# Two slots of the last expert stage shared between two experts, 96 rows of one and 32 of the other

## The chip, the cores and the metric

The kernel runs on one core of a Trainium2 chip. The time is device microseconds of that core; the kernel before takes 881.44 us (median of three runs, 881.35 to 882.75). All arithmetic is in float32. A float32 matrix product is two passes in the trace: two weight loads (PEld) and two matmuls (PE) for one product in the code.

## The reference, cut to what matters

An attention block feeds a mixture of experts in which each row goes to exactly one of eight experts, and no row is dropped.

```python
# attention: batch 8, 8 heads, 576 positions, head size 64; a window of 32,
# in half of the heads with steps of 4
attn = softmax(where(mask, q @ k.T / 8, -1e9));  x = (attn @ v)   # -> 4608 rows of 512
# experts: 8, hidden 1024
logits = x @ w_gate
expert_idx = np.argmax(logits, axis=1)
gate_w = softmax(logits)[row, expert_idx]
for e in range(E):                       # lo, hi: the rows of expert e, sorted
    h = np.maximum(x_sorted[lo:hi] @ w1[e], 0.0)     # 512 -> 1024
    y_sorted[lo:hi] = h @ w2[e]                      # 1024 -> 512
out = gate_w[:, None] * y                # in the rows' own order
```

How many rows an expert gets is known only when the kernel has computed the logits.

## The kernel before, in words

The kernel is one program in which two streams of work are interleaved as the program is written out: attention, with routing after each batch, and the expert slots.

**Buckets.** After the attention of a batch, `route` finds the expert of each of its 576 rows and its place among that expert's rows (VectorE, and small products on TensorE), and GpSimd scatters the rows by indirect DMA into `bucket` in HBM, in which expert e has the rows from e x 4608 on (L158). A row is 514 numbers: 512 of x, the gate's weight, the number of the token. After the last batch, GpSimd also writes blank rows behind the last row of each expert.

**Slots.** A slot is 128 consecutive rows of one expert's bucket. An expert whose count is no multiple of 128 has a last slot that is only partly filled. The number of slots is at most `NSLOT` = 43; the first 36 (`SURE`) always run, the others stand under a branch (L733) on the number that the tables found. Slots are planned in seven stages, one after each batch from the second on: `tables(s)` counts, on one partition of VectorE, the whole slots that are ready, and writes for each slot of the stage its expert (`ex`), the first row in the bucket (`base`), and whether its weights differ from those two slots before (`new`). The last stage, from slot 24 on, takes all that is left, partly filled slots too: experts are sorted by slots left, the list is cut in two halves, and even slots take the first half, odd slots the second, so that one expert stays in one of the two weight buffers.

**A slot's work** (`moe`). `across` turns the slot's 128x512 rows with four transposes (L721) and a copy on VectorE (L723). The first product keeps 128x128 pieces of w1 stationary and streams the 128 turned rows, 32 products into two PSUM banks (L747); ScalarE (L757) and VectorE (L765) apply the relu and so have the hidden layer already turned. The second product keeps pieces of that stationary and streams 512 columns of w2, 8 products (L771). ScalarE scales by the gate (L775), and GpSimd scatters the result rows to `out` (L780). The transposes of the next slot stand between the two halves of the first product.

**Loads.** w1 and w2 of an expert are 2 MB each, and each has two buffers, for even and odd slots. `wanted` is the list of loads in order: rows and w1 of slot j once slot j-2 is past its first product, w2 once slot j-2 is done. They are all issued from SP's queue, in this order; an issue waits on SP until the buffer's last reader is done (slot j-2), and all behind it wait too. A weight DMA has a condition (L695): where `new` is 0 it moves nothing.

**Order.** `run_slots` and `run_routing` set the program order: steps of a slot have costs written by hand (0.93, 0.88, 0.5), routing and tables proceed by one `yield` each time slots have advanced by 2.0 once attention is over.

## Time and profile before

| | |
|---|---|
| median of three runs | 881.44 us |
| the profiled execution | 879.85 us |
| its span, first to last instruction | 878.0 us |
| granted TensorE clock, mean | 0.956 |
| TensorE busy | 805.5 us (92%) |
| VectorE, ScalarE, GpSimd busy | 289.3, 224.9, 145.3 us |
| first product L747 | 2496 passes, 307.7 us |
| second product L771 | 624 passes, 294.2 us |
| slots that run (L775) | 39, the last one's y at 859.39 us |
| HBM read, written | 216.56 MB, 22.07 MB |

A page gives, for each group of instructions, the line of the program, the engine, the output and inputs by their names, the shape, the count, the busy time and the mean duration of one in ns, and the idle time before it with what ended it. Passes on TensorE overlap, so the mean duration of one (279 ns for L747) is longer than the distance from one to the next. PEclk is the granted clock in 40 slices of the span (9 is 0.9 or more). A timeline row is start, duration, engine, line and count of merged instructions, all in us. The issue of a DMA on SP's queue is marked SPq.

### The profile page before, as it was taken

The page shows a single profiled execution, that of the slowest core. Times are in us where ns is not written, and L with a number is a line of the kernel's source. Part 1 is how long each engine was busy: PE and PEld are TensorE (multiplying, and loading weights), DVE is VectorE, ACT ScalarE, POOL GpSimd, SP SyncE. Part 2 cuts the span into 40 slices and gives each one's busy share as a digit, 9 for nine tenths or more (in the row PEclk, how much of TensorE's full clock was granted, in tenths as well). Part 3 has the DMA queues.
Part 4 walks back from the last instruction along what each step waited for, and adds up shares of the span by engine and source line. Part 5 has one row for each costly group of instructions (what it writes and reads, how often), then busy time and mean ns, then how long its engine had stood idle before and what let it go on. Part 6 is the DMA issues. An engine that isn't in the chain of part 4 may idle for free.

```text
span 878.0 us, 17811 instructions
## 1 busy us (share of the span) xinstructions
PE 805.5 (92%) x6830; PEld 602.8 (69%) x6830; DVE 289.3 (33%) x891; ACT 224.9 (26%) x823; POOL 145.3 (17%) x139
## 2 busy tenths in 40 slices
PE   5888779899999999998999899889999999999991
PEld 4766668676677677776777677556867677777770
DVE  3775867445433433343334412310101010101010
ACT  3665463431433133332323121000000000000000
POOL 0214323213110311122111210420000000000000
PEclk9978889899999999999999899979999999999996
DMA  9877489898996869784367256769911380649574
GB/s 195 178 162 150 135 265 305 200 322 259 277 343 208 286 165 291 283 254 158 74 216 252 84 201 232 278 221 332 320 41 49 125 313 27 234 136 333 205 253 176
DMA packets 145720, 187.41 MB, mean 213 GB/s; under 512 B 72222, under 2 KB 86174, under 8 KB 145632
## 3 DMA queue, kind: packets, MB, share of 16 engines
q1 hardware_dynamic: 135316, 164.56, 61.6%
q0 software_dynamic: 6832, 19.71, 6.4%
q10 hardware_dynamic: 3484, 1.96, 1.0%
q8 instruction: 57, 0.93, 0.4%
q14 instruction: 31, 0.25, 0.1%
HBM read 216.56 MB, written 22.07 MB: 272 GB/s over the span
## 4 chain that ended last, share of the span: by engine, by line
PE 50%; issue 33%; DVE 4%; ACT 3%; POOL 3%; DMA 3%; another core or an unknown queue 1%; POOLq 0%; SPq 0%
PE ph L747 16%; PE py L771 15%; PE xo L340 4%; PE scores L274 4%; PE weights L325 3%; ACT e L300 3%; POOL out_dram L780 2%; PE xrow L426 2%; PE turned L238 2%; PE logits L436 2%; DMA k<-in_k_dram 2%; PE turned L246 1%; PE xt L721 1%; DMA bucket<-rows,idx 1%; POOL bucket L158 1%
## 5 line engine op out<-in xcount | busy, mean ns | idle before, releaser
L747 PE MATMUL ph<-xt,w 128*128 128x128 f32 x2496 | 307.7, 279 | 1.4 <-issue 1.4
L747 PEld LDWEIGHTS ph<-xt,w 128*128 128x128 f32 x2496 | 293.8, 193 | 20.7 <-issue 17.7
L771 PE MATMUL py<-w,h 128*128 128x512 f32 x624 | 294.2, 608 | 8.1 <-issue 8.1
L771 PEld LDWEIGHTS py<-w,h 128*128 128x128 f32 x624 | 112.7, 193 | 120.9 <-issue 116.7
L300 ACT ACTIVATE e<-e,lo 128x96 f32<-128x96 f32 x288 | 103.8, 364 | 91.9 <-DVE lo L294 84.7
L780 POOL DMA_INDIRECT out_dram<-y,to x39 | 38.8, 994 | 422.2 <-ACT y L775 388.7
L775 ACT ACTIVATE y<-py,x 128x512 f32<-128x512 f32 x39 | 26.7, 686 | 273.6 <-PE py L771 166.0
L723 DVE COPY xt<-xt 128x512 f32<-128x512 f32 x40 | 27.6, 690 | 210.0 <-PE xt L721 208.2
L315 POOL TENSOR_TENSOR e<-e,rec 128x864 f32<-128x864 f32 x32 | 52.1, 1629 | 202.6 <-DVE rec L314 107.1
L327 DVE COPY eT<-weights 96x384 f32<-96x384 f32 x96 | 48.4, 547 | 61.7 <-PE weights L325 54.3
L285 DVE SCALAR_TENSOR_TENSOR e<-scores,cst 128x384 f32<-128x384 f32 (+1 forms) x128 | 46.8, 396 | 48.2 <-PE scores L274 39.9
L765 DVE TENSOR_SCALAR h<-ph 128x512 f32<-128x512 f32 x39 | 27.0, 692 | 98.5 <-PE ph L747 86.3
L340 PEld LDWEIGHTS xo<-eT,v 96*64 96x64 f32 x1216 | 41.9, 143 | 24.0 <-issue 11.8
L274 PE MATMUL scores<-kT,qT 64*64 64x96 f32 x1152 | 43.4, 279 | 14.4 <-issue 8.3
L340 PE MATMUL xo<-eT,v 96*64 96x64 f32 (+1 forms) x1216 | 48.6, 231 | 6.6 <-issue 3.7
L300 ACT ACTIVATION_READ_ACCUMULATOR e<-e,lo 128x1 f32 x288 | 54.5, 189 | 0.0
L158 POOL DMA_INDIRECT bucket<-rows,idx x48 | 44.5, 928 | 57.3 <-DVE idx L525 26.9
L274 PEld LDWEIGHTS scores<-kT,qT 64*64 64x64 f32 x1152 | 34.6, 154 | 26.1 <-issue 16.0
L757 ACT ACTIVATE h<-ph 128x512 f32<-128x512 f32 x39 | 23.2, 596 | 102.4 <-PE ph L747 102.4
L325 PE MATMUL weights<-ident,e 128*96 128x128 f32 x288 | 42.1, 297 | 4.5 <-POOL e L315 4.5
L325 PEld LDWEIGHTS weights<-ident,e 128*96 128x96 f32 x288 | 35.1, 138 | 11.8 <-issue 5.2
L294 DVE TENSOR_REDUCE lo<-e 128x9 f32<-128x864 f32 x32 | 33.6, 1051 | 0.9
(104 smaller groups left out, 449.4 us busy)
## 6 DMA issues: line engine op xcount, KB each, us to landing
w<-in_moe_w_dram SPq DMA_DIRECT2D x82, 2048.0 KB
x<-bucket SPq DMA_DIRECT2D x41, 257.0 KB
v<-in_v_dram SPq DMA_DIRECT2D x32, 192.0 KB
q<-in_q_dram SPq DMA_DIRECT2D x32, 144.0 KB
q<-in_q_dram SPq DMA_DIRECT2D x8, 576.0 KB
v<-in_v_dram SPq DMA_DIRECT2D x48, 96.0 KB
k<-in_k_dram SPq DMA_DIRECT2D x28, 144.0 KB
k<-in_k_dram SPq DMA_DIRECT2D x7, 576.0 KB
```

Source lines behind the costliest of these rows:

```text
L158: nc.gpsimd.indirect_dma_start(out=bucket, out_offset=bass.IndirectOffsetOnAxis(ap=idx, axis=0), in_=rows, in_offset=None, bounds_check=NR ...
L274: nc.tensor.matmul(sc[r][64 * c : 64 * c + 64, 96 * (i % 5) : 96 * (i % 5) + 96], lhsT=qT[rows, 64 * j : 64 * j + 64], rhs=kT[rows, first_ ...
L285: nc.vector.scalar_tensor_tensor(out=e[p0:p1, i : i + n].rearrange("p i k -> p (i k)"), in0=sc[r][p0:p1, cols], scalar=-SCALE, in1=const(f ...
L294: nc.vector.tensor_reduce(out=lo, in_=e, axis=AX, op=OP.min)
L300: nc.scalar.activation(out=e[:, n], in_=e[:, n], func=AF.Exp, bias=lo[:, n : n + 1], scale=-1.0, accum_out=den[:, n : n + 1],)
L315: nc.gpsimd.tensor_tensor(out=e, in0=e, in1=rec.unsqueeze(2).broadcast_to([128, 9, 96]), op=OP.mult)
L325: nc.tensor.transpose(tp[0:96, 128 * i : 128 * i + 128], e[:, a + i], ident)
L327: nc.vector.tensor_copy(eT, tp[0:96, 0:384])
L340: nc.tensor.matmul(xo[DH * h : DH * h + DH, at0 : at0 + nq], lhsT=vt[:, 2 * hl + r, j, :] if ty == 0 else vt[:, hl, j, DH * r : DH * r + D ...
L747: nc.tensor.matmul(ph[:, fi], lhsT=w1[:, c, 128 * f : 128 * f + 128], rhs=xt[:, c], start=c == 0, stop=c == 3,)
L771: nc.tensor.matmul(py, lhsT=h[:, f], rhs=w2[:, f], start=f == 0, stop=f == 7)
L780: i = nc.gpsimd.indirect_dma_start(out=out, out_offset=bass.IndirectOffsetOnAxis(ap=to, axis=0), in_=y, in_offset=None, bounds_check=N - 1 ...
```

## The change

Groups of 32 rows become the unit in which the tails of experts are counted. `pairs` looks for experts with a tail of exactly one group; up to two of them (as many as there are other tails to go with) are each paired with the expert that has the largest tail. A pair shares one slot: 96 rows (three groups) of the one, 32 of the other. The two places for such slots are fixed: slots 24+3 and 24+7. `mixing` puts the experts and first rows of these slots in place of what the tables had. Where no pair is found, the same program computes nothing but rows of the first expert in that slot. `NSLOT` becomes 41.

A mixed slot is computed the other way round: the turned rows are stationary in four pieces of 32 columns, and w1 of the group's expert is streamed, 512 columns at a time, so each group of 32 rows comes out on its own 32 partitions (`grouped`). The hidden layer then has to be turned (`turned_h`, four transposes and a copy, twice). The second product is grouped likewise. The second expert's weights lie in the other parity's buffer; they are loaded when the slot before is past it, and the slot after the mixed one loads its own weights when the mixed slot is past it. From slot 26 on, rows are fetched from ScalarE's queue, in a mixed slot with four DMAs of 32 rows. The small constants of the last stage come with a DMA of their own on ScalarE's queue into a tile that attention no longer needs. The two buffers of w1, and those of w2, become one tile with an index.

```diff
+G = 32
+KIND = (3, 3)
+NMIX = len(KIND)
...
-NSLOT = (N + E * 127) // 128
...
+NSLOT = _most_slots()
...
+MIX = (3, 7)
+STEP = MIX[1] - MIX[0]
+J0 = STAGES[-1][1]
+assert J0 + MIX[-1] < SURE
...
+        if last:
+            scratch = pool.tile([TT, NT, 4, DH], F32, tag="q0", name="scratch", bufs=1)
+            scratch = scratch.rearrange("p t h d -> p (t h d)")[0:1]
+            width = packed_last.shape[1]
+            nc.scalar.dma_start(
+                scratch[:, 0:width], nc.inline_tensor(packed_last, name="c_last").ap()
+            )
+            mix["const"] = lambda name: scratch[:, last_at[name][0] : sum(last_at[name])]
+            used_up = [width]
...
+        if last:
+            yield
+            yield from pairs(cnt, table)
+            ns = mix["ns"]
...
+            plan, lists = table("plan", 2 * K, NMIX + 1), table("lists", 2 * K)
+            nc.vector.tensor_tensor(
+                out=plan,
+                in0=mix["const"]("plan").rearrange("p (k m) -> p k m", m=NMIX + 1),
+                in1=mix["many"].unsqueeze(1).broadcast_to([1, 2 * K, NMIX + 1]),
+                op=OP.mult,
+            )
+            nc.vector.tensor_reduce(out=lists, in_=plan, axis=AX, op=OP.add)
...
+            yield from mixing(ex, base, new, table)
...
+    def pairs(cnt, table):
+        c31, qi, qf = table("c31", E, dt=I32), table("qi", 2, E, dt=I32), table("qf", 2, E)
+        nc.vector.tensor_scalar(c31, cnt[0:1], G - 1.0, None, op0=OP.add)
+        nc.vector.tensor_scalar(qi[:, 0], c31, 5, None, op0=OP.logical_shift_right)
+        nc.vector.tensor_scalar(qi[:, 1], c31, 7, None, op0=OP.logical_shift_right)
+        nc.vector.tensor_copy(qf, qi)
...
+        ones, n1 = table("ones", E), table("n1", 1)
+        has, some = table("has", E), table("tails", 1)
+        nc.vector.tensor_scalar(ones, u, 1.0, None, op0=OP.is_equal)
+        nc.vector.tensor_reduce(out=n1, in_=ones, axis=AX, op=OP.add)
+        nc.vector.tensor_scalar(has, u, 1.0, None, op0=OP.min)
+        nc.vector.tensor_reduce(out=some, in_=has, axis=AX, op=OP.add)
...
+        nc.vector.tensor_scalar(rb, mix["const"]("ends"), some, None, op0=OP.add)
+        nc.vector.tensor_tensor(out=valid, in0=ra, in1=rb, op=OP.is_lt)
+        nc.vector.scalar_tensor_tensor(
+            out=valid, in0=ra, scalar=n1, in1=valid, op0=OP.is_lt, op1=OP.mult
+        )
+        nc.vector.tensor_reduce(out=m, in_=valid, axis=AX, op=OP.add)
+        nc.vector.tensor_scalar(many, mix["const"]("many"), m, None, op0=OP.is_equal)
...
+        nc.vector.tensor_tensor(out=ns, in0=has, in1=qf[:, 1], op=OP.add)
+        nc.vector.tensor_tensor(out=ns, in0=ns, in1=paired, op=OP.subtract)
+        yield
+        mix.update(ns=ns, m=m, many=many, valid=valid, got=got)
...
+    def mixing(ex, base, new, table):
+        valid = mix["valid"]
...
+        other, newb = mixf[:, 0:NMIX], mixf[:, NMIX : 2 * NMIX]
+        instead(other, at(ex, MIX[0]), b[0], "inex")
+        instead(at(ex, MIX[0]), at(ex, MIX[0]), a[0], "inex")
+        nc.vector.tensor_copy(prev, exs[:, J0 - 2 : NSLOT - 2])
+        nc.vector.tensor_copy(at(prev, MIX[0] + 1), other)
+        nc.vector.tensor_tensor(out=newb, in0=other, in1=at(ex, MIX[0] - 1), op=OP.not_equal)
+        nc.vector.tensor_tensor(out=new, in0=ex, in1=prev, op=OP.not_equal)
...
+        for i, n in enumerate(KIND):
+            own = mix["const"]("own")[:, 4 * i : 4 * i + 4]
+            for x, g0, g1 in ((first, 0, n), (then, n, 4)):
+                nc.vector.tensor_scalar(
+                    begins[:, i, g0:g1], own[:, g0:g1], x[:, i : i + 1], None, op0=OP.add
+                )
+        mixi = mpool.tile([1, 6 * NMIX], I32, name="mixi", bufs=1)
+        nc.vector.tensor_copy(mixi, mixf)
+        mix["ints"] = mixi
...
-    w1s = [cpool.tile([128, 4, F], F32, name=f"w1_{i}") for i in range(2)]
-    w2s = [cpool.tile([128, 8, DM], F32, name=f"w2_{i}") for i in range(2)]
+    w1s = cpool.tile([128, 2, 4, F], F32, name="w1")
+    w2s = cpool.tile([128, 2, 8, DM], F32, name="w2")
+    mixed = {J0 + at0: i for i, at0 in enumerate(MIX)}
...
+        queue = nc.scalar if j >= J0 + 2 else nc.sync
+        if j in mixed:
+            for g in range(4):
+                a = 2 * NMIX + 4 * mixed[j] + g
+                at0 = queue.value_load(
+                    mix["ints"][:, a : a + 1], min_val=0, max_val=NROWS - G
+                )
+                read_bucket(queue.dma_start(x[G * g : G * g + G], bucket[ds(at0, G), :]), b)
+        else:
+            at0 = queue.value_load(basei[:, n : n + 1], min_val=0, max_val=E * CAP)
+            read_bucket(queue.dma_start(x, bucket[ds(at0, 128), :]), b)
+    def fetch_w(j, dst, src, other=False):
         _, n, exi, _, newi = where[j]
-        rv = nc.sync.value_load(exi[:, n : n + 1], min_val=0, max_val=E - 1)
+        if other:
+            i = mixed[j]
...
-            dst[j % 2], src[ds(rv, 1)].rearrange("o (c l) f -> l (o c) f", l=128), **kw
+            dst[:, (j + other) % 2], src[ds(rv, 1)].rearrange("o (c l) f -> l (o c) f", l=128), **kw
...
-        wanted += [(j, "x", 0, j - 1), (j, "w1", 0, j - 1), (j, "w2", 1, j - 1)]
+        x = (j, "x", 0, j - 1)
+        behind = j - (j - 1 not in mixed)
+        w = [(j, "w1", 0, behind), (j, "w2", 1, behind)]
+        if j - 1 in mixed:
+            wanted.insert(len(wanted) - 1, x)
+        else:
+            wanted.append(x)
+        wanted += w
+        if j in mixed:
+            wanted += [(j, "w1b", 0, j), (j, "w2b", 1, j)]
...
+            def grouped(out, lhsT, ws, cols, c, n, j=j):
+                for g in range(4):
+                    mine = slice(G * g, G * g + G)
+                    nc.tensor.matmul(
+                        out[mine],
+                        lhsT=lhsT[:, mine],
+                        rhs=ws[:, (j + (g >= KIND[mixed[j]])) % 2, c, cols],
+                        start=c == 0,
+                        stop=c == n - 1,
+                    )
+            def turned_h(hrow, fg):
+                ps = bank("ht", 4, 128)
+                for fi in range(4):
+                    nc.tensor.transpose(ps[:, fi], hrow[:, fi], ident)
+                (nc.scalar.copy, nc.vector.tensor_copy)[fg](h[:, 4 * fg : 4 * fg + 4], ps)
+            hrows = []
+            for fg in range(2) if j in mixed else ():
+                ph = bank("ph")
+                for c in range(4):
+                    grouped(ph, xt[:, c], w1s, slice(512 * fg, 512 * fg + 512), c, 4)
+                    if (fg, c) == (1, 1):
+                        turned_h(hrows[0], 0)
+                    yield 0.93
+                hrow = mpool.tile([128, 4, 128], F32, tag="xt", name="hrow")
+                flat = hrow.rearrange("p i f -> p (i f)")
+                if fg == 0:
+                    nc.scalar.activation(flat, ph, AF.Relu)
+                    while late:
+                        late.pop(0)()
+                else:
+                    nc.vector.tensor_scalar(flat, ph, 0.0, None, op0=OP.max)
+                    done[0] = j + 1
+                    fetch()
+                hrows.append(hrow)
...
+                if j in mixed:
+                    if f == 2:
+                        turned_h(hrows[1], 1)
+                    if f == 4 and j + 1 in xs:
+                        nxt = across(j + 1)
+                    grouped(py, h[:, f], w2s, slice(0, DM), f, 8)
+                else:
+                    nc.tensor.matmul(py, lhsT=h[:, f], rhs=w2[:, f], start=f == 0, stop=f == 7)
```

## The prediction

> **What bounds the kernel now.** I read the page first, then the order of time on each engine at the end of the kernel, then the DMA issues there.
>
> ```profile
> span 878.0 us, 17811 instructions
> PE 805.5 (92%) x6830; PEld 602.8 (69%) x6830; DVE 289.3 (33%) x891; ACT 224.9 (26%) x823; POOL 145.3 (17%) x139
> PEclk9978889899999999999999899979999999999996
> L747 PE MATMUL ph<-xt,w 128*128 128x128 f32 x2496 | 307.7, 279 | 1.4 <-issue 1.4
> L771 PE MATMUL py<-w,h 128*128 128x512 f32 x624 | 294.2, 608 | 8.1 <-issue 8.1
> ```
>
> TensorE is the bound, and 602 of its 805 us are two lines, the first and second product of the expert slots. 624 instructions on L771, 16 in a slot, mean that 39 slots run. In the order of time on TensorE every slot after 585 us looks like this one:
>
> ```profile
> 599.04 3.73 PE L747 MATMUL ph<-xt,w 128*128 128x128 f32 x32
> 602.62 0.60 PE L721 MATMUL xt<-ident,x 128*128 128x128 f32 x4
> 603.05 3.74 PE L747 MATMUL ph<-xt,w 128*128 128x128 f32 x32
> 606.63 7.03 PE L771 MATMUL py<-w,h 128*128 128x512 f32 x16
> 613.50 3.73 PE L747 MATMUL ph<-xt,w 128*128 128x128 f32 x32
> ```
>
> A slot takes 613.50 - 599.04 = 14.46 us with no gap: 7.59 for the first product with the four transposes, 6.87 for the second (0.43 a pass, two passes for a float32 product). Slots 20 to 38 stand so, 19 in a row. A slot removed from this tail is worth 14.46 us if nothing else gets in the way.
>
> **How many slots go.** The reference on its inputs sends 592, 502, 602, 499, 669, 476, 540 and 728 rows to the experts. In groups of 32, rounded up, what lies over whole slots of 128 is 3, 0, 3, 0, 1, 3, 1, 3 groups. Two experts (4 and 6) have a one-group tail, so both pairs are valid: 0 with 6 in slot 24+3 = 27, 2 with 4 in slot 31. 39 slots become 37: **-28.9 us**.
>
> **What a mixed slot costs TensorE.** It streams the weights (512 columns, two passes of 0.43) past four stationary pieces of 32 columns, 8 times in each product. If the four run side by side, that is 16 x 0.86 = 13.74 us; one after the other it would be 55. The trace has no group of four 32-column pieces, but near rows:
>
> ```profile
> 444.23 1.04 PE L274 MATMUL scores<-kT,qT 64*64 64x96 f32 x36
> 445.20 1.13 PE L771 MATMUL py<-w,h 128*128 128x512 f32 x2
> ...
> 454.27 0.82 PE L426 MATMUL xrow<-ident,xT 128*96 128x128 f32 x6
> 455.02 0.53 PE L436 MATMUL logits<-xT,wg 128*32 128x192 f32 x6
> 455.48 0.66 PE L721 MATMUL xt<-ident,x 128*128 128x128 f32 x4
> ```
>
> L436 is nearly the new form: 128 rows by 32 columns, three column places, each with its own moving data. A pass of 192 columns at the rate of L771 (512 in 0.43) is 0.161 us; six alone would be 0.97, and the next work starts after 0.46. So three ran side by side (two rounds of 0.161, and 0.14 around them). L274 puts 36 passes of 96 columns (0.08 each, 2.9 alone) into 0.97 us in four quarters of the array, the two halves of its rows with them. I take full overlap of four: 13.74. Against this stands the Trainium skill, "TensorE: Matmul & The Clock Gate", Part 3: three column tiles with 512 moving columns measured only 2.38 times as fast. At that efficiency (2.38/3) a group costs 1.08 instead of 0.86, and 32 groups in two slots 7 us more. The row decides, since it is this program's own stream; the 7 us go to the range.
>
> Besides there are 8 transposes more (0.11 each by L721: 0.88), the usual four (0.44), and four stretches of column work between transposes, which cost 0.09 going in (455.02 - 454.27 less six times 0.11) and 0.14 coming out, 0.92 in all. The copies of the turned rows (0.6 to 0.7 each, as L757 and L765) have 1.7 us of passes as cover. Sum 15.98, 1.5 above a plain slot: **+3.0 us** for two.
>
> **What it costs in weights.** This speaks most against the change. A mixed slot's second expert goes into the buffer that the slot before still reads and the slot after needs, so three loads follow one another where there was one. From the rules that place the experts, the old tail loads slots 20-24, 29, 30, 33, 35, 36, 37. The queue of SP agrees: a long issue (0.37 us) moves data, a short one (0.08) is skipped.
>
> ```profile
> 693.52 7.25 SPq L696 DMA_DIRECT2D w<-in_moe_w_dram  x2
> 707.97 7.25 SPq L696 DMA_DIRECT2D w<-in_moe_w_dram  x2
> 722.42 0.08 SPq L696 DMA_DIRECT2D w<-in_moe_w_dram  x1
> ```
>
> After the change the experts by slot from 24 are 7, 6, 7, 0+6, 0, 7, 1, 2+4, 5, 3, 5, 4, 6, and loads are needed for 24, 25, 27 (twice), 28, 29, 30, 31 (twice), 32, 33, 35, 36: 33 pairs in the program for 27. How fast they go is in the DMA rows of 690 to 725 us (40 slices of 0.875 us):
>
> ```profile
> DMA  0000098999990959999997889999558999999910
> GB/s 19 0 0 0 0 112 239 379 412 435 407 389 23 110 176 405 398 377 382 403 387 171 145 300 440 412 412 412 243 77 136 274 372 393 332 401 410 350 66 0
> ```
>
> About 1 us from issue to the first bytes, a ramp, 380 to 435 in between, some 1.2 us of tail. At 390 to 410, 2.1 MB take 5.1 to 5.4 us; with a slot's rows in and out (0.5 MB, 1.3 us), 12.0 us for a pair, of which I give w1 5.4 and w2 6.6. The Trainium skill ("DMA: Bandwidth & Descriptors", Specifications) has about 358 GB/s as the HBM limit of one core; the trace goes above it, so I keep 400. By the page a pair with its rows is 13.2 us.
>
> Now the order. w1 of expert 6 for slot 27 can be issued when slot 26 ends its first product, 6.87 us before it is needed, and takes 1.05 + 5.4 + 1.2 = 7.65: TensorE waits 0.8. Its w2 is late by 0.3. From the end of slot 27 the queue never empties: w2 of 28, both of 29, 30 and 31, then w1 of expert 4. The first lands after 1.05 + 6.6 + 1.2 = 8.85 and is needed after 7.59: 1.3 late. The last lands after 1.05 + 6.6 + 3 x 12.0 + 5.4 + 1.2 = 50.3; slots 28 to 30 end at 1.3 + 43.4 = 44.7. So **slot 31 waits 5.6 us**; slot 32 again 1.3. Sum **+9.3 us**. With 11.2 a pair it is 4.9, with 13.2 it is 15. The second expert's load stands last in the queue, so every slice of bandwidth counts there. A wait of 5 us also costs clock, as the stretches after two old gaps show (columns: stretch, length, busy time of PE, PEld, DVE, ACT, POOL, granted clock, DMA share, GB/s):
>
> ```profile
> 497.00:504.00 7.00, 5.65 (x28) 5.34 (x29) 2.56 (x6) 0.60 (x1) 0.15 (x1) 0.53 0.14 52
> 569.00:583.00 14.00, 8.54 (x10) 2.79 (x10) 2.21 (x11) 0.00 (x0) 5.29 (x6) 0.51 0.38 117
> ```
>
> Half clock for about 7 us, part of it in the wait: **+2.5 us**, 0 to 3.5.
>
> **What I cost at nothing.** The last stage's tables get about 50 more VectorE instructions on one row. Their kind takes 0.13 to 0.39 us there now, so about 10 us; the tables end at 581 us now, and the first row fetch that needs them belongs to slot 24, after slot 22's first product at 584.6 + 2 x 14.46 + 7.6 = 621. Cover 40 us; without it, up to 10. The constants' load on ScalarE's queue is small (1 us to first bytes, as above); behind its first reader on VectorE stands the relu of slot 19, and who waits for that is TensorE, which crawls there anyway (8 passes of L771 between 564 and 579). The row fetches on ScalarE's queue (one register load and one DMA, four each in a mixed slot, about 1.2 us each) lie between relu and y, 10 us apart. For slots 29 and 33 the fetch stands behind y of the mixed slot: 2.0 for y and issue, 1.05, and 1.5 of shared transfer make 4.6 us, for a transpose at 3.6. That 1 us is taken from the wait for w2 that follows it, so nothing is added. The end (859 to 878: last scatter and four skipped slots) keeps its four.
>
> **Sum**: -28.9 + 3.0 + 9.3 + 2.5 = -14.1 on the profiled execution's 879.85 (1.85 more than its span). The median of the runs is 881.44, so 867.3; I say **867**.
>
> **Rivals.** (1) *Loads hidden better*: the queue holds 410 throughout, stalls 4.9 and no lost clock: 881.4 - 28.9 + 3 + 5 = 860.5. The slices of 412 speak for it, those of 330 to 380 against. (2) *Bandwidth or array by the page*: 13.2 a pair costs 6 us more, 873; 2.38-fold overlap 7 more, 874; both, 880. (3) *Slower*: four column pieces do not overlap fully. 14.1 us of gain over 32 groups is 0.44 a group, so at 1.30 us a group (overlap of 2.6) nothing is left; at two at a time (1.72) it is 867 + 27.5 = 895. L436 and L274 speak against; no row has four pieces of 128 rows and 512 columns. (4) *Nothing is paired*: about 881. It takes a count off by a few rows at a border of 32; the queue's pattern above fits the counts.
>
> **Chances.** The likeliest case (863 to 872) 0.55, (1) 0.15, (2) 0.17, (3) 0.10, (4) 0.03. Leaving out the slow case and half of the extremes gives 858 to 878. A change under 0.2% (1.8 us) can't be told from none; faster 0.87, same 0.03, slower 0.10.
>
> **What would show it.** L771 with 560 passes of the old form (35 slots) and 37 y's; passes of 32 columns starting in fours; a mixed slot of 16 us without its waits; a wait of 4 to 8 us of TensorE before slot 31 ended by a weight DMA, with half clock after it; waits of 1 us near 27, 28 and 32. The forecast is wrong if the passes start singly, if slot 31 starts on time or over 10 us late, or if TensorE stands between 585 and 621 us for a table.

## The result, and the profile after

The changed kernel takes 869.84 us (median of four runs, 868.38 to 873.2) against 881.39 us for the kernel before on the same chip: a ratio of 0.9873 [0.9842, 0.9903]. The forecast was 867. In later runs, on a chip where the kernel before takes 880.02 us, the ratio is 0.9903 [0.9882, 0.9925]. On another, where it takes 842.18 us, it is 0.9978 [0.9958, 0.9999]. So the size of the gain depends on the chip, which nothing in the forecast allowed for; the experiments say why. A ratio is taken over the fast runs of both kernels, with its 95% interval in brackets, and differs by up to 0.33% from the quotient of the two medians.

The page of the changed kernel (its lines have moved: the first product is L1023, the second L1054, the grouped product of a mixed slot L985):

```profile
span 871.3 us, 17722 instructions
PE 789.7 (91%) x6774; PEld 571.6 (66%) x6774; DVE 292.6 (34%) x938; ACT 223.6 (26%) x821; POOL 143.7 (16%) x137
PEclk9987979899999999999999989969999998999996
L1054 PE MATMUL py<-w,h 128*128 128x512 f32 x560 | 268.9, 616 | 14.1 <-issue 5.3
```

There are 560 passes of the second product: 35 plain slots and two mixed ones, 37 in place of 39. The clock row (a digit is 21.8 us) has an 8 at 719 to 741 us, where the row of before has a 9; that is slot 28, below. The 6 further left is slot 19, where before has a 7.

The end of the kernel is compared best from the output of slot 21 to that of the last slot, because what lies before it differs from chip to chip and this stretch hardly does (236.37, 236.39 and 237.00 us in three traces of the changed kernel). I call it **the tail**. Before it is 859.39 - 613.75 = 245.64 us; after, 853.04 - 616.67 = 236.37. That is 9.3 us less, where 14.1 were forecast. (The profiled execution is the slowest of the four, and the output of its first slot comes 3 us later than before; the tail does not contain that.) The order of time on TensorE shows slots 27 (mixed) and 28:

```profile
688.92 1.90 PE L985 MATMUL ph<-w,xt 128*32 128x512 f32 x8
691.25 5.34 PE L985 MATMUL ph<-w,xt 128*32 128x512 f32 x40 [0.43 <-DMA w<-in_moe_w_dram]
696.52 0.66 PE L996 MATMUL ht<-ident,hrow 128*128 128x128 f32 x4
...
704.60 0.66 PE L959 MATMUL xt<-ident,x 128*128 128x128 f32 x4
705.19 3.64 PE L985 MATMUL py<-w,h 128*32 128x512 f32 x32
708.76 3.84 PE L1023 MATMUL ph<-xt,w 128*128 128x128 f32 x32
712.44 0.60 PE L959 MATMUL xt<-ident,x 128*128 128x128 f32 x4
712.87 3.74 PE L1023 MATMUL ph<-xt,w 128*128 128x128 f32 x32
719.52 10.18 PE L1054 MATMUL py<-w,h 128*128 128x512 f32 x16 [2.91 <-DMA w<-in_moe_w_dram]
729.54 1.72 PE L1023 MATMUL ph<-xt,w 128*128 128x128 f32 x14
```

Read the row at 705.19 first: 32 passes of 512 columns in 3.57 us (to 708.76). That is eight rounds of four, 0.43 each and 0.13 around them. The four groups run side by side at full rate. Then the first two rows: TensorE waits for the second expert's w1, but the row puts only 0.43 us down as idle. Passes of the other groups run ahead, so the wait hides in rounds that are not full; the 48 passes last 696.52 - 688.92 = 7.60 us, and 5.29 where the weights are there in time (below). Last the row at 719.52: 2.91 us of wait for slot 28's own w2, then 16 passes in 10.18 us instead of 7.03. The stretch around it (columns: stretch, length, busy time of PE, PEld, DVE, ACT, POOL, clock, DMA share, GB/s):

```profile
716.00:727.00 11.00, 8.09 (x17) 3.60 (x16) 1.39 (x3) 0.00 (x0) 0.00 (x0) 0.69 1.04 403
```

The DMA engines are full at 403 GB/s, and the clock is halved for 6.8 us of the 11 (granted 0.69).

### The profile page after: what moved, and what is told of

It is laid out like the page before. It is cut to its first block, busy times and chain, and to the rows that moved or that the text cites. A ratio compares the mean times of both kernels' runs of the same rounds, so it can differ in the third digit from the quotient of the medians.

```text
span 871.3 us, 17722 instructions
## 1 busy us (share of the span) xinstructions
PE 789.7 (91%) x6774; PEld 571.6 (66%) x6774; DVE 292.6 (34%) x938; ACT 223.6 (26%) x821; POOL 143.7 (16%) x137
## 4 chain that ended last, share of the span: by engine, by line
PE 51%; issue 32%; DVE 4%; DMA 4%; POOL 3%; ACT 3%; another core or an unknown queue 1%; POOLq 0%; SPq 0%; ACTq 0%; DVEq 0%
PE ph L1023 16%; PE py L1054 15%; PE xo L386 4%; PE scores L320 4%; PE weights L371 4%; ACT e L346 2%; POOL out_dram L1063 2%; PE xrow L472 2%; DMA k<-in_k_dram 2%; PE logits L482 2%; PE turned L284 2%; PE turned L292 1%; PE xt L959 1%; DVE e L331 1%
## 5 line engine op out<-in xcount | busy, mean ns | idle before, releaser
L1054 PE MATMUL py<-w,h 128*128 128x512 f32 x560 | 268.9, 616 | 14.1 <-issue 5.3
L1023 PE MATMUL ph<-xt,w 128*128 128x128 f32 x2240 | 277.7, 279 | 1.7 <-issue 1.7
L1023 PEld LDWEIGHTS ph<-xt,w 128*128 128x128 f32 x2240 | 264.2, 193 | 19.9 <-issue 17.0
L1054 PEld LDWEIGHTS py<-w,h 128*128 128x128 f32 x560 | 101.7, 195 | 115.2 <-issue 105.8
L1063 POOL DMA_INDIRECT out_dram<-y,to x37 | 36.9, 997 | 413.7 <-ACT y L1058 380.1
L386 PEld LDWEIGHTS xo<-eT,v 96*64 96x64 f32 x1216 | 42.1, 145 | 20.1 <-issue 8.1
L204 POOL DMA_INDIRECT bucket<-rows,idx x48 | 44.7, 931 | 57.5 <-DVE idx L571 26.9
L1041 DVE TENSOR_SCALAR h<-ph 128x512 f32<-128x512 f32 x35 | 24.2, 690 | 63.8 <-PE ph L1023 56.0
L1060 DVE CAST to<-x 128x1 int32<-128x1 f32 x37 | 5.4, 147 | 119.5 <-DMA out_dram<-y,to 78.3
L1033 ACT ACTIVATE h<-ph 128x512 f32<-128x512 f32 x35 | 20.9, 596 | 93.4 <-PE ph L1023 81.6
L371 PEld LDWEIGHTS weights<-ident,e 128*96 128x96 f32 x288 | 35.7, 140 | 11.5 <-issue 6.4
```

The lines of the kernel that those rows point to most:

```text
L204: nc.gpsimd.indirect_dma_start(out=bucket, out_offset=bass.IndirectOffsetOnAxis(ap=idx, axis=0), in_=rows, in_offset=None, bounds_check=NR ...
L371: nc.tensor.transpose(tp[0:96, 128 * i : 128 * i + 128], e[:, a + i], ident)
L386: nc.tensor.matmul(xo[DH * h : DH * h + DH, at0 : at0 + nq], lhsT=vt[:, 2 * hl + r, j, :] if ty == 0 else vt[:, hl, j, DH * r : DH * r + D ...
L1023: nc.tensor.matmul(ph[:, fi], lhsT=w1[:, c, 128 * f : 128 * f + 128], rhs=xt[:, c], start=c == 0, stop=c == 3,)
L1054: nc.tensor.matmul(py, lhsT=h[:, f], rhs=w2[:, f], start=f == 0, stop=f == 7)
L1063: i = nc.gpsimd.indirect_dma_start(out=out, out_offset=bass.IndirectOffsetOnAxis(ap=to, axis=0), in_=y, in_offset=None, bounds_check=N - 1 ...
```

## The experiments

The runs were made in five groups, each on one chip. The kernel before takes 881.39 and 880.02 us in two of them, and 841.34, 841.76 and 842.18 in the others, on three chips; I speak of the 881 kind and the 842 kind. Ratios are therefore to the kernel before on the same chip; slot lengths (from output to output) are from the profiled execution, in us. The kernel before was profiled on the first chip only. In the three kernels whose mixed slots are 26 and 31 (e_mix27, e_fix27, e_best), the column "27, 28" has slots 26 and 27.

| kernel | tail | 27, 28 | 31, 32 | 19 + 20 | median, before | ratio |
|---|---|---|---|---|---|---|
| before | 245.64 | 14.45, 14.44 | 14.46, 14.45 | 43.07 | 881.39 | |
| changed | 236.37 | 19.87, 20.84 | 19.43, 17.17 | 43.09 | 869.84, 881.39 | 0.9873 [0.9842, 0.9903] |
| a_again (changed) | 236.39 | 19.79, 19.33 | 19.61, 18.75 | 43.09 | 871.07, 880.02 | 0.9903 [0.9882, 0.9925] |
| a_third (changed) | 237.00 | 20.09, 19.16 | 19.57, 18.92 | 35.90 | 841.16, 842.18 | 0.9978 [0.9958, 0.9999] |
| e_noload | 222.30 | 17.07, 14.61 | 16.07, 14.61 | 37.16 | 825.72, 841.34 | 0.9782 [0.972, 0.9844] |
| e_split | 223.19 | 16.12, 14.62 | 18.52, 14.61 | 36.10 | 826.32, 841.34 | 0.979 [0.9723, 0.9858] |
| e_mix27 | 234.64 | 17.31, 18.60 | 19.99, 18.83 | 35.72 | 837.01, 841.34 | 0.9937 [0.9904, 0.997] |
| e_xsync | 245.20 | 18.54, 24.80 | 18.79, 24.13 | 29.49 | 842.19, 841.34 | 0.9977 [0.9951, 1.0002] |
| e_gate | 236.70 | 20.02, 18.31 | 19.90, 18.87 | 43.10 | 873.66, 880.02 | 0.9926 [0.9898, 0.9953] |
| e_gate2 | 237.00 | 19.63, 19.39 | 19.84, 18.78 | 29.49 | 832.80, 841.76 | 0.987 [0.9824, 0.9916] |
| e_late | 240.48 | 20.13, 20.01 | 19.66, 18.78 | 33.47 | 843.95, 841.76 | 1.0006 [0.9983, 1.0028] |
| e_fix | 223.45 | 16.16, 14.62 | 18.39, 14.62 | 43.11 | 856.62, 880.02 | 0.9731 [0.9709, 0.9753] |
| e_fix27 | 221.45 | 16.08, 14.61 | 16.52, 14.74 | 43.06 | 854.58, 880.02 | 0.969 [0.9652, 0.9728] |
| e_best | 221.16 | 16.07, 14.62 | 16.44, 14.88 | 29.49 | 815.57, 841.76 | 0.9673 [0.9639, 0.9708] |

### What the second expert's weights cost: e_noload

All four groups of a mixed slot use the first expert's weights; the second expert's are not loaded, the slot after needs no reload, and its rows are fetched in their usual place in the list again. The 32 rows of the other expert in each mixed slot are thus multiplied with the wrong weights.

```diff
-                        rhs=ws[:, (j + (g >= KIND[mixed[j]])) % 2, c, cols],
+                        rhs=ws[:, j % 2, c, cols],
...
-        behind = j - (j - 1 not in mixed)
+        behind = j - 1
...
-        if j in mixed:
-            wanted += [(j, "w1b", 0, j), (j, "w2b", 1, j)]
```

> All four groups of a mixed slot read the slot's own weights: the second expert's weights are not loaded, and the slot after a mixed one keeps what its buffer holds. Leaves out: the 32 rows of the second expert in each mixed slot get the first expert's weights. All TensorE work stays. Theory (the loads are the whole loss): 881.4 - 28.9 + 3 = 855.5 us, within 2. Rival (something else in the change costs: the longer tables, the rows from ScalarE's queue, the grouped passes): clearly above 858.

The tail falls from 236.4 to 222.3: 14.1 us hang on these loads. But the ratio, 0.9782, would be 862 us on the first chip (857 to 868), more than the 855.5 that the loads alone would leave. What costs besides lies ahead of the tail, in the column of slots 19 and 20, and is taken up below. What is left of waits in the tail is on VectorE: 0.93 us in slot 27, and 0.33 in slot 30.

```profile
666.06 1.90 PE L978 MATMUL py<-w,h 128*32 128x512 f32 x16
668.89 0.66 PE L989 MATMUL ht<-ident,hrow 128*128 128x128 f32 x4 [0.93 <-DVE hrow L1007]
```

Without it slot 27 would be 16.1, as slot 31 is (16.07). The grouped arithmetic costs 16.1, whatever the weights do.

### The same loads, begun earlier: e_split

The loads of a mixed slot's second expert, and of the slot after it, are issued as two halves. The first half waits only for the half of the buffer that it overwrites.

```diff
-        nc.sync.dma_start(
-            dst[:, (j + other) % 2], src[ds(rv, 1)].rearrange("o (c l) f -> l (o c) f", l=128), **kw
-        )
+        to = dst[:, (j + other) % 2]
...
+        for a in range(2):
+            if src is moe_w1:
+                half = src[ds(rv, 1), :, 512 * a : 512 * a + 512]
+                part = to[:, :, 512 * a : 512 * a + 512]
+            else:
+                half = src[ds(rv, 1), 512 * a : 512 * a + 512, :]
+                part = to[:, 4 * a : 4 * a + 4]
+            nc.sync.dma_start(part, half.rearrange("o (c l) f -> l (o c) f", l=128), **kw)
```

> The four weight loads at each mixed slot (w1 and w2 of the second expert, w1 and w2 of the slot after) are each issued as two halves, the half that is read first going first. Theory (each load comes too late by its own length, 8.8 to 10.9 us from issue to landing against 6.9 to 7.6 us of cover): a half waits only for the half product that read its part of the buffer, so it goes out 3 to 4 us earlier and is half as long; the waits at slots 27, 28, 31 and 32 (12.7 us in the profile of after) and the half clock (3 us) go, 855 to 859 us, mixed slots of 16.0 us. Rival (the bandwidth of the queue, the backlog of my prediction): the bytes are the same, so a wait of 5 us or more stays at slot 31, 862 to 868.

The tail is 223.2, within 0.9 us of not loading at all, with all rows computed by the right expert. Slots 27, 28 and 32 are at their length without waits. What remains is at slot 31 (18.5), 2.4 us where the rival expected 5 or more. The ratio alone (0.979, which would be 857 to 869 us on the first chip) could not have told the two apart; it has the 36.1 us of slots 19 and 20 in it. Here is the same stretch in e_fix, which has these halves too (below):

```profile
686.70 5.36 PE L1003 MATMUL ph<-w,xt 128*32 128x512 f32 x48
691.99 0.66 PE L1014 MATMUL ht<-ident,hrow 128*128 128x128 f32 x4
...
702.83 3.84 PE L1041 MATMUL ph<-xt,w 128*128 128x128 f32 x32
706.51 0.60 PE L977 MATMUL xt<-ident,x 128*128 128x128 f32 x4
706.95 3.74 PE L1041 MATMUL ph<-xt,w 128*128 128x128 f32 x32
710.52 7.03 PE L1076 MATMUL py<-w,h 128*128 128x512 f32 x16
```

The 48 passes run through in 5.29 us, and slot 28's w2 is there: no wait and full clock. There the first half of the second expert's w1 is issued at 675.92, once slot 26 has used the first half of its w1, the other at 679.93; their last packets end at 684.20 and 686.91, and the slot starts at 686.70. In the changed kernel the whole was issued at 682.15, for a start at 688.92: 6.8 us of cover for a load that took 8.8 to its last packet.

### Mixed slots further apart: e_mix27

```diff
-MIX = (3, 7)
+MIX = (2, 7)
```

> The first mixed slot is moved from the fourth place of the stage to the third, slot 26. The plan then puts the second expert (6) into slot 25 as well, so its weights lie in the right buffer already and are not loaded; slot 27 loads its own expert anew. 31 pairs of loads instead of 33. Theory (each load late by its own length): slot 26 lasts 16 us instead of slot 27's 19.9, the slot after still waits 2 to 3 us for its w2, slot 31 waits 2.5 and 1 us as before: 864 to 867. Rival (backlog): fewer pairs ahead of slot 31 take its waits away as well: 860 to 863.

The tail gains 1.7 us over the first trace of the changed kernel, 2.4 over a_third, which is from a chip of the same kind. Against a_third, slots 26 and 27 together are 3.3 us shorter than 27 and 28 were, 31 and 32 are 0.3 longer, and slot 30 waits 0.6. Waits of the old size stay at slots 27, 31 and 32 (2.04 us for a weight in slot 27): more room between the mixed slots gives no load more cover of its own.

### Rows from SP's queue: e_xsync

```diff
-        queue = nc.scalar if j >= J0 + 2 else nc.sync
+        queue = nc.sync
```

> All rows are fetched from SP's queue again, the rest as after. The rows of slots 29 and 33 then stand behind the w2 of slots 28 and 32 in one queue. Theory (a queue works in order, so they land after that w2, some 11 us after the mixed slot's end, and are needed after 3.6): TensorE waits 6 to 7 us at the transposes in the middle of the first product of slots 28 and 32 in place of 2.9 and 2.3 us later; 874 to 880. Rival (queues share the same engines, so it makes no difference from where a row is fetched): 868 to 872, as after.

The tail goes back to 245.2, so ScalarE's queue is worth 8.2 (a_third) to 8.8 us there. In slot 28 the rows of slot 29 now stand behind a weight load that waits for its buffer:

```profile
681.29 1.08 PE L959 MATMUL xt<-ident,x 128*128 128x128 f32 x4 [7.21 <-DMA x<-bucket]
682.17 6.10 PE L1023 MATMUL ph<-xt,w 128*128 128x128 f32 x32
```

But the time, 842.19, is nowhere near 8 us above the changed kernel's on such a chip (841.16). The column of slots 19 and 20 says where the difference went: they take 29.5 us here, and 35.7 to 37.2 in the three kernels above, on the same chip. What comes before the tail had been left out of these expectations, and the next five runs are about it.

### ScalarE's register loads: a_again, e_gate, e_gate2, e_late, a_third

A row fetch needs its first row in a register of the engine that issues it. In the trace of the changed kernel, the register loads for slots 26 to 37 don't stand beside their fetches. They come in one block, 18 of them, most 0.56 us apart, as soon as the last stage's table is written: 7 of them ahead of the first relu of slot 20 on ScalarE, 11 behind it. In e_noload one of them stands even ahead of the output of slot 19, so that its 37.16 us divide into 21.94 and 15.22.

Two runs repeat the changed kernel on other chips.

> The changed kernel again, on whichever chip this is. Theory (its row fetches put their register loads on ScalarE ahead of slot 20's relu, and that costs 6 to 7 us wherever TensorE does not crawl through slot 19 anyway): on a chip where the kernel before takes about 841 us, slots 19 and 20 together last 36 us instead of 29.5, the stretch from the output of slot 21 to that of the last slot stays 236.4 us (245.6 before), and the ratio is 0.997; where it takes about 881 us, slots 19 and 20 together last 43 in both and the ratio is 0.987. Rival (the loads are hidden everywhere): ratio 0.987 to 0.989 on any chip.

It came on a chip of the 881 kind: tail 236.39, slots 19 and 20 43.09, as theory and rival alike had it there. The one for the other kind is a_third:

> The changed kernel once more, for a chip on which the kernel before takes about 841 us. Theory (register loads ahead of slot 20's relu cost 6.2 to 7 us there): slots 19 and 20 last 36 us together, ratio 0.995 to 0.998, some 6 us above the kernel whose loads are held back (0.987 there). Rival: 29.5 us and 0.987. Where the kernel before takes about 881 us both expect 43 us and 0.987 to 0.990.

Slots 19 and 20 last 35.90 and the ratio is 0.9978, as the theory said. Seven register loads stand ahead of the relu of slot 20 in a_third (count, then shortest, median and longest in ns, then first and last start), and ScalarE and TensorE in that slot show what comes of it:

```profile
L908 ACTq TENSOR_LOAD <-basei x3: 277/282/467, 553.9 to 557.6; - x3
L903 ACTq TENSOR_LOAD <-mixi x4: 277/282/289, 554.8 to 556.5; - x4
```

```profile
546.84 0.69 ACT L1058 ACTIVATE y<-py,x 128x512 f32<-128x512 f32 x1 [10.27 <-PE py L1054]
558.24 0.60 ACT L1033 ACTIVATE h<-ph 128x512 f32<-128x512 f32 x1 [10.71 <-issue]
```

```profile
546.59 3.73 PE L1023 MATMUL ph<-xt,w 128*128 128x128 f32 x32
550.16 0.60 PE L959 MATMUL xt<-ident,x 128*128 128x128 f32 x4
550.60 3.74 PE L1023 MATMUL ph<-xt,w 128*128 128x128 f32 x32
558.89 8.73 PE L1054 MATMUL py<-w,h 128*128 128x512 f32 x16 [4.56 <-ACT h L1033]
```

The relu (558.24) usually comes 3.57 us after the y before it, so it was due at 550.41 and is 7.83 us late. The table is written at 553.9, 3.5 us after that; the seven loads are the rest, 4.3 us. The "issue" in brackets is how the trace shows waits of ScalarE's sequencer. TensorE has 3.2 us of slack, then idles 4.56, then needs 8.73 us for passes that take 7.03 at full clock (granted 0.59 from 558 to 562).

In e_gate and e_gate2 (the same kernel on two chips) the loads are held back: they read copies of the tables that also depend on the relu of slots 23 and 24.

```diff
+    def release(name, ints, h):
+        z = mpool.tile([1, 1], F32, name=f"z_{name}", bufs=1)
+        nc.vector.tensor_scalar(z, h[0:1, 0, 0:1], 0.0, None, op0=OP.mult)
+        rows[name] = mpool.tile([1, ints.shape[1]], I32, name=f"late_{name}", bufs=1)
+        nc.vector.tensor_scalar(rows[name], ints, z, None, op0=OP.add)
...
                     nc.scalar.activation(h[:, 0:4], ph, AF.Relu)
+                    if j == J0 - 1:
+                        release("basei", where[J0][3], h)
+                    if j == J0:
+                        release("mixi", mix["ints"], h)
```

> The changed kernel, with the register loads of ScalarE's row fetches held back to the stretches after the first relu of slots 23 and 24, by a data dependence, where ScalarE waits some 10 us for the next output. Theory: slots 19 and 20 last 29.5 us together where the kernel before takes 841 us, the stretch from slot 21 on stays 236.4, so the ratio goes to 0.989 there, 6 to 7 us under the changed kernel; no gain over it (1.4 us at most) where before takes 881. Rival: no difference from the changed kernel on any chip; or the loads in their new place hold up an output and slot 23 or 24 grows by 1 us or more.

> The changed kernel with the loads held back to slots 23 and 24, once more. Theory: if TensorE does not crawl through slot 19 on this chip (kernel before about 841 us), slots 19 and 20 last 29.5 us and the ratio is 0.989, where the changed kernel's would be 0.997; if it does (about 881 us), 43.1 us and 0.99 as before. Rival: 36 us for the two slots also here, so that the stall comes from something else than the loads.

On the chip of the 881 kind nothing is won (0.9926 against 0.9903, intervals overlapping). Slot 24 grows by 0.9 us: the copy that releases the loads comes late, because VectorE stands until 651.39 for a row fetch, and y then stands behind the loads; 0.25 of it is made up in slot 25. On the other kind the ratio goes from 0.9978 (a_third) to 0.987 [0.9824, 0.9916] on another chip of that kind, and slot 20 is whole (e_gate2):

```profile
548.55 0.69 ACT L1071 ACTIVATE y<-py,x 128x512 f32<-128x512 f32 x1 [10.27 <-PE py L1067]
552.13 0.60 ACT L1042 ACTIVATE h<-ph 128x512 f32<-128x512 f32 x1 [2.89 <-PE ph L1032]
```

```profile
552.31 3.74 PE L1032 MATMUL ph<-xt,w 128*128 128x128 f32 x32
555.88 7.03 PE L1067 MATMUL py<-w,h 128*128 128x512 f32 x16
```

Last, the stall made on purpose: in e_late the loads for slots 26 to 33 are written (as `ahead`) in front of the first relu of slot 24, and depend on the output of slot 23.

```diff
+                    if j == J0:
+                        ahead()
                     nc.scalar.activation(h[:, 0:4], ph, AF.Relu)
...
+            if j == J0 - 1:
+                release("basei", where[J0][3], y)
+                release("mixi", mix["ints"], y)
```

> The changed kernel, with 16 of ScalarE's register loads made to run between the output of slot 23 and the first relu of slot 24, a place without crawl on every chip. Theory (16 loads of 0.56 us and the wait for the release before them hold the relu 6.7 us; it has 3.2 us of slack before TensorE needs it; TensorE then idles 3.5 us and runs some 7 us at half clock): slot 24 lasts 20 to 21 us instead of 14.5, the stretch from slot 21's output to the last becomes 242 to 243 instead of 236.4, the time 6 us above the changed kernel's. Rival (the loads run beside the relu or are hidden): slot 24 stays 14.5 us and the time is the changed kernel's.

```profile
611.29 0.69 ACT L1083 ACTIVATE y<-py,x 128x512 f32<-128x512 f32 x1 [10.28 <-PE py L1079]
620.87 0.60 ACT L1058 ACTIVATE h<-ph 128x512 f32<-128x512 f32 x1 [8.89 <-issue]
```

```profile
615.05 3.74 PE L1046 MATMUL ph<-xt,w 128*128 128x128 f32 x32
621.52 7.13 PE L1079 MATMUL py<-w,h 128*128 128x512 f32 x16 [2.73 <-ACT h L1058]
```

The stall is there, and half of what was expected: TensorE idles 2.73 us rather than 3.5, and the clock stays full. The loads in that place are 14 (slots 26 to 33), not the 16 that I had counted, and the relu is 6.0 us late. Slot 24 takes 17.40, 2.95 more than a plain slot, not 6. In slot 20 four loads are left that wait for the table, and it takes 18.43 us, with half clock: with seven loads in front of its relu slot 20 is 6.4 us longer (a_third), with four 4.0, with none not at all (e_gate2). So the loads in front of a relu do cost TensorE time, and the delay of the relu less about 3 us of slack is the price; what the clock adds depends on where the gap falls (last section).

### Together: e_fix, e_fix27, e_best

e_fix has the halves and the loads held back; e_fix27 also has its mixed slots at 26 and 31; e_best is e_fix27 on another chip.

> Both mendings: register loads held back, and the loads around the mixed slots issued in halves. Theory: the two are independent, so the stretch from slot 21 on lasts 223 us as with halves alone, and slots 19 and 20 last 29.5: 22 us under the kernel before on any chip, ratio 0.974. Rival (what is won in one place is lost in the other, since both act on the same queue's start): 0.979 as with halves alone.

> As the run before it, but with the mixed slots five apart instead of four (26 and 31). Theory (the wait of 2.4 us left at slot 31 is the queue's backlog of six changes of expert in a row, each pair about 10.5 us): one more slot of cover of 14.45 us removes it, so slot 31 falls from 18.5 to about 16 us and the ratio to 0.971. Rival (the plan's other order of experts brings as many new pairs in front of slot 31): no difference, 0.974.

> Loads in halves, register loads held back, mixed slots at 26 and 31, as run before: the ratio to the kernel before 0.969, within 0.004, on any chip; the stretch from slot 21's output on 221.5 us.

The parts add up. The tail of e_fix is 223.45, as with halves alone. Its one wait for a weight is at slot 31, and there the queue is the cause: the first half of the second expert's w1 is issued at 735.60, and its first packet moves at 743.68, behind the loads before it. These stretches of e_fix show the DMA engines meanwhile:

```profile
730.00:735.00 5.00, 5.00 (x34) 3.92 (x33) 0.00 (x0) 0.69 (x1) 0.98 (x1) 1.00 1.04 400
735.00:740.00 5.00, 5.00 (x44) 4.76 (x43) 0.27 (x2) 0.60 (x1) 0.00 (x0) 1.00 1.03 403
740.00:745.00 5.00, 5.00 (x13) 2.13 (x12) 1.10 (x2) 0.00 (x0) 0.00 (x0) 1.00 1.04 387
```

They are full for 15 us, and slot 31 still waits. With one slot more in between (e_fix27) its wait is nearly gone; first e_fix, then e_fix27:

```profile
746.38 1.92 PE L1003 MATMUL ph<-w,xt 128*32 128x512 f32 x12
748.72 5.34 PE L1003 MATMUL ph<-w,xt 128*32 128x512 f32 x36 [0.43 <-DMA w<-in_moe_w_dram]
753.99 0.66 PE L1014 MATMUL ht<-ident,hrow 128*128 128x128 f32 x4
```

```profile
745.80 5.81 PE L1003 MATMUL ph<-w,xt 128*32 128x512 f32 x48
751.54 0.66 PE L1014 MATMUL ht<-ident,hrow 128*128 128x128 f32 x4
```

7.61 us for the 48 passes become 5.74. The move that was worth 1.7 to 2.4 us without halves (e_mix27) is worth 2.0 with them, in another place. e_best takes 815.57 us against 841.76: 0.9673 [0.9639, 0.9708], with the kernel of e_fix27 at 0.969 [0.9652, 0.9728] on the other kind of chip. It beats both kernels on both kinds.

## Why the prediction was right, and where it was wrong

**Two slots fewer, -28.9: right.** There are 37 outputs, and plain slots take 14.45 before and after. Rival 4 falls with that.

**A mixed slot's arithmetic, 15.98: right.** The full overlap of four groups was read from L436 and L274, against the page's 2.38 for three tiles (the Trainium skill, "TensorE: Matmul & The Clock Gate", Part 3). The runs measure 0.43 us a round of four, so full overlap, and 16.07 us a slot where nothing waits (e_noload slot 31, e_best slot 26). Rivals 2 (the part of it on the array) and 3 fall with that.

**The weight waits, +9.3 and +2.5 of clock: right in kind, too small, and in the wrong slots.** The lengths of slots 27, 28, 31 and 32 sum to 77.3, where 2 x 15.98 and 2 x 14.45 would be 60.9: 16.5 us, not 11.8. Of this 3.2 is clock (10.18 us in slot 28 for passes of 7.03), and 13.3 is waits. By slot, with the clock in it, the forecast had 1.1, 1.3, 8.1 and 1.3; measured were 3.9, 6.4, 3.5 and 2.7. In the two repeats the sum is the same (16.6 and 16.9), but slots 28 and 32 share it otherwise (4.9 and 4.3 in a_again), since the clock falls elsewhere. Two terms failed:

- **The time of one load.** I had 7.65 us from issue to the last packet for the first w1 and 8.85 for w2 of slot 28; they took 8.8 and 10.0. The load before that w1 was still moving until 684.09, and from 684 to 690 the core's DMA moved 326 GB/s, where I had counted on 390 to 410. The cover was as computed (6.8 us), so each of these two waits grew by about one and a half us, and the half clock that I had put behind slot 31 came in slot 28.
- **The backlog of 5.6 us at slot 31.** It rested on 12.0 us a pair. At full rate a pair takes 10.5 (the last packet of w2 of slot 28 ends at 718.91, those of 29 at 724.04 and 729.45; 403 GB/s). Put into the forecast's own sum, 1.05 + 6.6 + 3 x 10.5 + 5.4 + 1.2 = 45.8 against 44.7, the wait would be 1.1. Slot 28 had also lost 6.4 us where the sum has 1.3, which gave the queue time: in the changed kernel the second w1 for slot 31 is issued at 751.76, finds only the end of one load before it (754.67), and ends after 8.8 us, as in slot 27. The backlog only comes out when the other waits are gone (e_split, e_fix: 2.3 to 2.4 us there). The page's 358 GB/s ("DMA: Bandwidth & Descriptors", Specifications), which I kept for rival 2, is not the limit here: the full stretches moved 387 to 403.

The 2.5 us of clock rested on "half clock for about 7 us" in two old stretches; the second of them, 569 to 583, shows 14 us of it. That the clock's cost came near the forecast is luck: whether a wait is followed by half clock depends on how it falls in time (last section).

**What I costed at nothing: wrong for the row fetches.** The step said that register loads and fetches "lie between relu and y, 10 us apart", and that the table's first reader is a row fetch at 621 us. In fact its first reader on ScalarE is a register load, at 588 us in that profile, ahead of slot 20's relu; the fetches themselves do lie where I said. On the profiled chip this cost hardly anything: that relu is 1.4 us late, within TensorE's slack, and slot 20 takes 14.45. But this is so because slot 19 there takes 28.64 us rather than 15.04, so that the table is written as slot 20 begins (588.1) and not 7 us into it (a_third). That was the cover, and on chips of the 842 kind it is not there: 6.4 us (35.90 against 29.49), most of the gain that was left. That TensorE stands for a table was named as a sign that the forecast is wrong, between 585 and 621 us; slot 20 is the first slot of that stretch. On the first chip the sign did not show; on the other kind it does, 7 us into the slot.

**The sum.** -14.1 was forecast, and the tail shows -9.3; of the 4.8 between them the weight waits and their clock make 4.7. The median of the runs moved by 11.5 on the first chip and 9.0 on the second, so part of the agreement with 867 lies in the spread of the runs. Part of it is luck with the chip: on a chip of the 842 kind the median moved by 1.0 (a_third), where the forecast would have missed by 13. Rival 1, loads hidden better, failed in the direction of it: they were hidden worse.

## What to carry to other kernels

When a load is only late by the time that its buffer is held, issue it in pieces that follow its readers: here two halves won 13 of 14 us, more than the placing of the slots. A load into a register is an instruction in its engine's order; look where it stands in that order, not where its use stands, and what work of that engine is behind it. And a cost that is hidden by a delay which belongs to the chip and not to the program is hidden on that chip only; name the cover, and price its absence.

## What was not expected of the hardware

- **Groups of columns proceed on their own.** While the fourth group lacks its weights, passes of the others run on and then stop, and the fourth is made up for alone. In slot 31 of e_fix the 12 passes before the wait start in four rounds of three, and the 36 behind it take 5.27 us, where nine rounds of four would take 3.9 and the fourth group's own twelve passes 5.2. So the trace shows 0.43 us of idle time for a wait that costs 2.3, in slot 27 as in slot 31, and running ahead gains almost nothing.
- **Chips differ in a few places of this program.** Slot 19 takes 28.6 us on chips of the 881 kind, and 15.0 on those of the 842 kind (the 21.9 in e_noload are the register loads, see above). Slots 2, 6, 11 and 16 are likewise longer on the first kind, by 3 to 8 us, and the first output comes 5 to 16 us later; slot 3 is shorter there (20.1 against 22.3 to 30.6). Why is open; no run was aimed at it. In slot 19 of the changed kernel VectorE stands still for 7.67 us until 581.51, and TensorE for 3.46 behind it, while the trace names no cause.
- **The half clock comes in windows of 3.4 us, and a wait is followed by it or not according to how it falls on them.** Within a trace of these runs its starts lie whole multiples of 3.41 us apart, and it lasts one such window or several (3.4 us in slot 27 of e_mix27, 6.8 in slot 28 of the changed kernel, 10.2 in slot 28 of e_xsync). Here are the two windows around the wait in slot 28 and the one behind them, first in the changed kernel, then in e_gate:

```profile
715.48:718.89 3.41, 1.13 (x11) 0.94 (x9) 1.39 (x3) 0.00 (x0) 0.00 (x0) 1.00 1.04 411
718.89:722.30 3.41, 2.78 (x4) 1.26 (x5) 0.00 (x0) 0.00 (x0) 0.00 (x0) 0.50 1.02 414
722.30:725.72 3.42, 3.42 (x6) 1.35 (x5) 0.00 (x0) 0.00 (x0) 0.00 (x0) 0.50 1.04 392
```

```profile
711.59:715.00 3.41, 1.87 (x17) 1.68 (x16) 0.29 (x2) 0.00 (x0) 0.00 (x0) 1.00 1.05 398
715.00:718.42 3.42, 1.50 (x4) 0.82 (x5) 1.08 (x2) 0.00 (x0) 0.00 (x0) 1.00 1.02 416
718.42:721.83 3.41, 3.41 (x10) 1.50 (x9) 0.00 (x0) 0.00 (x0) 0.00 (x0) 1.00 1.03 395
```

(TensorE's busy time stands behind the length, the granted clock third from the end.) The wait of 2.91 us left TensorE 1.13 us of work in one window and was followed by half clock; the longer wait of e_gate, 3.46 us, is divided over two windows with 1.87 and 1.50 us of work and was not. The other waits in the tails go the same way: 1.37 us of work in a window (e_mix27, slot 27, with 2.04 us of idle) were followed by half clock, 1.66 and 2.43 (e_late, slot 24, with 2.73) were not. So in these tails the border for a window at full clock lies between 1.4 and 1.5 us of work. I drew it after the fact and no run was aimed at it; ahead of the tail a window with 1.81 us of work (e_fix, at 565.94) was followed by half clock too. The Trainium skill ("TensorE: Matmul & The Clock Gate", Part 1) has windows of 3.4 us that run freely, and the traces agree with that.
